# Sums over the keys on halves of TensorE's columns, numerators on quarters, and late projections in float32 on half rows, in a linear-attention and gated-FFN kernel

## The chip, the cores and the metric

The kernel runs on one core of one Trainium2 chip. The metric is the device time of one execution in microseconds (us), taken as the median of several runs; less is better. The granted TensorE clock was 1.0 (full) over the whole profiled execution of the kernel before.

## The reference

Two stages follow each other. The first is linear attention over 8 batches of 8 heads, with 576 tokens and 64 channels a head. The second is a gated FFN on the 4608 tokens of 512 channels that come out of it. All is float32.

```python
def phi(x):                                   # 64 channels -> 2 * 128 features
    proj = x @ w_phi
    proj = proj - max(abs(proj), axis=-1)
    return concat([exp(proj), exp(-proj)])
q_p, k_p = phi(q), phi(k)
kv  = einsum('bhsf,bhsd->bhfd', k_p, v)       # sums over the 576 keys
z   = sum(k_p, over s)
attn = einsum('bhsf,bhfd->bhsd', q_p, kv) / (einsum('bhsf,bhf->bhs', q_p, z) + 1e-6)
x = attn as [4608, 512]
g = x @ w_gate                                # 512 -> 1536
out = (g * sigmoid(g) * (x @ w_val)) @ w_out  # 1536 -> 512
```

## The kernel before

**Work.** Attention goes by pairs of heads: 4 pairs a batch, 32 in all, each by a call of `attention(i, rank)` (L452). Pairs 0 to 11 are early, 12 to 31 late. The FFN goes by 12 chunks of 384 tokens. Four are done plainly (`first`, L838, and `second`, L904), eight in twos by a scheme with seven products in place of eight (`strassen`, L1085; its products stand in L1102). Each FFN product is three matmuls in fp32r, a float32 form that TensorE streams in one pass: operands are split into a high and a low part, and high by high, high by low and low by high are summed. The helper `matmuls` (L338) issues these, and others. A plain float32 matmul is one row in the program and two in the trace: two passes, each with a LDWEIGHTS of its own (L568 stands 192 times in the program and 384 times in the trace).

**A pair**, on TensorE. A form is given as rows*columns of the stationary operand, as in the profile.

- Projection of the keys: 576 tokens by `w_phi`. Early: float32, 64*128, four blocks of 128 tokens for each of two heads. A head has 64 channels, so one stands on rows 0 to 63 and the other on 64 to 127 (L516); the last 64 tokens of both heads go as one block of 128*128. Late: ScalarE rounds the keys to fp32r (L490), VectorE makes the low part (L492), and twelve matmuls of 128*128 with 256 moving columns against a block-diagonal weight follow, three for each block, and three for the rest (L527, issued in L338).
- VectorE subtracts the largest magnitude of each token (L536, L542), ScalarE makes both exponentials (L547). Then come the sums over the keys: features are stationary (128 tokens by 128 features), values and a column of ones move (65 columns). That is 16 float32 matmuls of 128*128 a pair, in two steps of eight (L568 early, L562 late), and two of 130 columns for the last tokens (L558). All go to one PSUM bank, which ScalarE copies out (L583).
- Projection of the queries. Early: 64*128 float32 (L605), then transposes (L627). Late: features come out on partitions at once. ScalarE rounds (L651), VectorE makes low parts (L653), and eight fp32r matmuls of 128*128 with 288 columns follow (L663, issued in L338); the largest magnitude is then found by VectorE transposes (L671 to L690).
- Denominators: 128*32, four column quarters (two heads by two halves of the tokens), 288 columns (L705). Numerators: 128*64, one head on each half of the columns, 288 columns, in two steps by halves of the tokens (L719).

**What sets the order.** Nothing above is issued where it stands. Each step is handed to `Plan.add` (L94) with its engine, an assumed cost, the steps that it waits for, a rank, and the PSUM banks that it takes and gives. `Plan.run` (L108) plays a list schedule at build time: a free engine takes the ready step of lowest rank. Attention has the pair's number as its rank and FFN products have 1001 and up, so they fill in wherever no attention step is ready. The instructions stand on the hardware's queues in the order that this play gives. If TensorE finds nothing ready in the play, `nothing` (L1292) puts in an idle matmul on zeros (L1297, L1299; 64*128, 256 columns). The assumed costs are `pe`, `pe32`, `dve`, `act` (L198 to L219) and 215 for a float32 matmul of the key sums (L571).

**Buffers.** Early pairs alternate between two sets of `qx`, `qe`, `kvs`. Late pairs keep high and low parts in `qx1` and `qe1` (L287, L288). From pair 15 on a second set of features lies in the tiles that the split of the FFN weights has left (`other_qe`, `other_qx`); `kvs1` alone serves late pairs, and `kvs0` and `wb` become tiles for FFN intermediates (`TH_TAGS`, L42). That split of the weights is `weight_piece` (L347): 36 pieces, with loads, VectorE and ScalarE work, between the early and the late pairs.

Of the kernel before, what the change touches and what calls it, by code (L numbers as in the profile page):

```python
# [17 lines left out]
P = 128  # L18
S = 576
# [22 lines left out]
TH_TAGS = ("kvs0", "wb", "w2_lo0", "w2_lo1")  # L42
# [3 lines left out]
SECOND_SET = 15  # L46
# [17 lines left out]
class Step:  # L64
    __slots__ = ("eng", "cost", "fn", "left", "then", "rank", "n", "lag", "take", "give", "key", "port", "slot", "drop")

    def __init__(self, eng, cost, fn, rank, n, lag, take, give, key):
        self.eng, self.cost, self.fn, self.rank, self.n, self.lag = eng, cost, fn, rank, n, lag
        self.take, self.give, self.key = take, give, key
        self.left, self.then, self.slot, self.drop = 0, [], None, []  # L70


class Plan:
# [5 lines left out]
    BYTES, ISSUE = 320.0, 420.0  # L79
# [14 lines left out]
    def add(self, eng, cost, fn, after=(), rank=0.0, take=None, give=None):  # L94
# [3 lines left out]
        s.port = port  # L98
        seen = set()
# [8 lines left out]
    def run(self):  # L108
# [6 lines left out]
        events, n, wire = [], 0, 0.0  # L115
        now = 0.0

        def start(e):
            nonlocal n, wire
# [13 lines left out]
            if got is None:  # L133
                if e == "PE" and self.fill is not None and any(ready.values()) | any(busy.values()):
                    cost = self.fill()
# [13 lines left out]
            if e in port:  # L149
                port[e] = s.port  # L150
            if e == "SP":
                wire = max(wire, now + self.ISSUE) + s.cost / self.BYTES
                freed, done = now + self.ISSUE, wire + s.lag
            else:
                freed, done = now + s.cost - (self.OVERLAP[e] if s.cost > 200 else 0), now + s.cost + s.lag
# [39 lines left out]
FILL = 150  # L195

# [26 lines left out]
def favor_attention_moe(ctx: ExitStack, tc: tile.TileContext, qT, kT, v, w_phi, wg, wv, wo, out):  # L223
# [18 lines left out]
    wbd_hi, wbd_lo = sb("wbd_hi", [P, 2 * NF], F32R), sb("wbd_lo", [P, 2 * NF], F32R)  # L242
    wst_hi, wst_lo = sb("wst_hi", [P, NF], F32R), sb("wst_lo", [P, NF], F32R)
# [55 lines left out]
    wb = sb("wb", [P, 3 * NF])  # L299
    wbd, wst = wb[:, :2 * NF], wb[:, 2 * NF:]  # L300
# [5 lines left out]
    for hi, lo, w in ((wbd_hi, wbd_lo, wbd), (wst_hi, wst_lo, wst)):  # L306
        nc.scalar.copy(hi, w)
        nc.vector.tensor_tensor(out=lo, in0=w, in1=hi, op=ALU.subtract)
# [105 lines left out]

    def rows(h):
# [36 lines left out]
    def attention(i, rank):  # L452
        b, pr = divmod(i, NPAIR)
        early = i < EARLY_PAIRS
        split = not early
        j = i % 2 if early else 0
        vec = nc.vector

        older = (i - 1, i - 2) if i == EARLY_PAIRS else (i - 2,) if early else (i - 1,)
        use = lambda name: [last.get((name, n)) for n in older]  # L460
        own = 0 if i < SECOND_SET else i % 2
        same = (i - 2,) if early else (i - 1, i - 2) if own == 0 else (i - 2,) if i > SECOND_SET + 1 else ()
        if not early and own == 0 and i >= SECOND_SET:
            same = (i - 2,) if i > SECOND_SET + 1 else (i - 1, i - 2)
        use_q = lambda name: [last.get((name, n)) for n in same] + (weights_done if own and not early else [])
        e_part = (lambda: qe[j]) if early or not own else other_qe
        x_part = (lambda: qx[j]) if early or not own else other_qx
        kj = j if early else 1

# [6 lines left out]
        q_in = add("SP", P * S * 4, lambda: nc.sync.dma_start(qin[j], qT[b, pr]), [last.get(("qin", n)) for n in ((i - 2,) if i < EARLY_PAIRS else (i - 1, i - 2))], rank)  # L476
# [10 lines left out]
        if early:  # L487
            k_ready = k_in
        else:
            k_hi = add("ACT", act(KW), lambda: nc.scalar.copy(k_parts()[:, 0], kin),  # L490
                       [*k_in, last.get(("khi", i - 1)), *(use("qx") if i == EARLY_PAIRS else ())], rank)
            k_lo = add("DVE2", dve(KW), lambda: vec.tensor_tensor(  # L492
                out=k_parts()[:, 1], in0=kin, in1=k_parts()[:, 0], op=ALU.subtract), [k_hi], rank)
            k_ready = [k_hi, k_lo]
            last["kin", i] = k_lo
        kv_steps = []
        ps_kv = lambda: work[plan.bank["kv", i]]
        for g, (t0, t1) in enumerate(K_GROUPS):
# [5 lines left out]
            by_head = early and not both  # L504
# [4 lines left out]
            def project(t0=t0, t1=t1, key=key, heads=heads, both=both):  # L509
                projected.append(1)  # L510
                o = work[plan.bank[key]]
                if early and not both:
                    for t in range(4):
                        for h in range(2):
                            o = work[plan.bank["k", i, h]]
                            nc.tensor.matmul(o[:, t * NF:(t + 1) * NF], kin[rows(h)[0], t * P:(t + 1) * P],  # L516
                                             wst[rows(h)[0]], start=True, stop=True)
                    return
                for t in range(t0, t1):
                    c = slice(t * P, (t + 1) * P)  # L520
                    acc = o[:, (t - t0) * heads * NF:(t - t0 + 1) * heads * NF]
                    if early:
                        matmuls([(acc, kin[:, c], wst, True, True)])
                    else:
                        khi, klo = (k_parts()[:, n, c] for n in range(2))
# [826 lines left out]
```

## Time and profile before

| | |
|---|---|
| Time, median of 3 runs | 1249.28 us (1248.83 to 1250.91) |
| The profiled execution's own time | 1248.93 us |
| Its span, first to last instruction | 1246.9 us |
| Busy: PE, PEld (weight loads) | 1237.0 us, 1092.0 us |
| Busy: DVE, ACT, POOL | 861.4 us, 616.6 us, 102.1 us |
| DMA over the span | 242 GB/s |

PE is TensorE's matmuls, PEld its weight loads, DVE VectorE, ACT ScalarE, POOL GpSimd. A busy time is a union of intervals with modelled ends, so neighbours overlap: how fast matmuls follow each other is read from start to start, in the timeline or in the chain that ended last, whose pieces lie end to end. Roughly, the early pairs lie in the first 183 us, the split of the weights up to 290 us, the late pairs with plain FFN chunks and the first seven-product chunks from 290 to 790 us, and FFN alone behind that.

### The profile page before, as it was taken

How to read it: one execution, taken by the hardware profiler on the slowest of the kernel's cores; microseconds unless marked ns; L12 is line 12 of the kernel's file. 1: busy time of each engine (PE TensorE's matmuls, PEld its weight loads, DVE VectorE, ACT ScalarE, POOL GpSimd, SP SyncE). 2: the span in 40 equal slices, each digit the busy share in tenths (PEclk: the TensorE clock that was granted, in tenths of full speed). 3: DMA queues.
4: the chain of work that ended last, by engine and by line, in shares of the span. 5: the costliest groups of instructions: out<-in, count | busy, mean ns of one | idle time of the engine just before them, and what ended most of it. 6: DMA issues, size and time to landing. Idle time of an engine off the chain costs nothing.

```text
span 1246.9 us, 22330 instructions
## 1 busy us (share of the span) xinstructions
PE 1237.0 (99%) x7857; PEld 1092.0 (88%) x7857; DVE 861.4 (69%) x1568; ACT 616.6 (49%) x1347; POOL 102.1 (8%) x108
## 2 busy tenths in 40 slices
PE   9999999999999999999999999999999999999998
PEld 8778889999988889877898988799988998899987
DVE  6888989989888888987988789324552447324441
ACT  5666663333476576666766656423333334323322
POOL 0000000000021332000000010001100111001100
PEclk9999999999999999999999999999999999999999
DMA  4543679988578999784967767879997999879865
GB/s 140 135 121 100 199 221 300 312 295 271 181 236 272 308 316 306 223 269 150 300 197 228 207 190 220 277 243 307 307 294 216 302 306 284 255 223 305 293 189 166
DMA packets 216559, 301.26 MB, mean 242 GB/s; under 512 B 61568, under 2 KB 121216, under 8 KB 216448
## 3 DMA queue, kind: packets, MB, share of 16 engines
q1 hardware_dynamic: 216128, 299.71, 75.8%
q8 instruction: 62, 1.02, 0.3%
q14 instruction: 49, 0.40, 0.1%
q10 hardware_dynamic: 320, 0.13, 0.0%
HBM read 221.12 MB, written 78.64 MB: 240 GB/s over the span
## 4 chain that ended last, share of the span: by engine, by line
PE 91%; DVE 5%; DMA 2%; issue 1%; ACT 1%; POOL 0%; SPq 0%; DVEq 0%; ACTq 0%; POOLq 0%
PE work L338 41%; PE work L1102 26%; PE work L562 6%; PE work L719 5%; PE work L568 4%; PE work L705 3%; PE work L558 1%; PE work L627 1%; PE work L516 1%; PE work L605 1%; PE work L1299 1%; DMA w_dram<-shared 1%; PE work L1297 1%; DMA shared<-in_wg_dram 0%; DMA m<-h_dram 0%
## 5 line engine op out<-in xcount | busy, mean ns | idle before, releaser
L338 PE MATMUL work<-w_hi,hh 128*128 128x512 f32 x468 | 182.8, 399 | 0.0
L1124 DVE TENSOR_TENSOR m<-m,work 128x384 f32<-128x384 f32 x144 | 78.5, 552 | 127.1 <-ACT m L1121 79.7
L338 PE MATMUL work<-w_hi,m 128*128 128x512 f32 x396 | 156.5, 395 | 0.0
L331 DVE TENSOR_TENSOR m<-m,hh 128x384 fp32r<-128x384 f32 x132 | 73.3, 567 | 102.8 <-ACT hh L895 98.6
L895 ACT CAST hh<-m 128x384 fp32r<-128x384 f32 x144 | 72.3, 511 | 128.2 <-PE work L338 106.8
L338 PE MATMUL work<-xh,w_big 128*128 128x384 f32 x384 | 133.6, 348 | 1.4 <-DVE m L868 1.3
L338 PE MATMUL work<-xl,w_big 128*128 128x384 f32 x384 | 128.7, 335 | 0.0
L1102 PE MATMUL work<-tb,stream_xh 128*128 128x384 f32 x618 | 113.9, 336 | 1.4 <-DVE m L1124 1.1
L331 POOL TENSOR_TENSOR m<-m,m 128x384 f32<-128x384 f32 x48 | 59.8, 1245 | 645.6 <-DVE m L1129 475.5
L1102 PEld LDWEIGHTS work<-tb,stream_xh 128*128 128x128 f32 x618 | 107.0, 188 | 3.8 <-DVE m L1124 1.7
L547 ACT ACTIVATE kp<-kp 128x512 f32<-128x512 f32 (+1 forms) x192 | 98.9, 523 | 19.1 <-DVE kp L542 16.4
L338 PEld LDWEIGHTS work<-w_hi,hh 128*128 128x128 f32 x468 | 87.9, 188 | 20.6 <-issue 0.9
L1128 ACT ACTIVATE m<-m 128x384 f32<-128x384 f32 x96 | 45.5, 518 | 122.0 <-DVE m L1124 122.0
L1121 ACT COPY m<-work 128x384 f32<-128x384 f32 x144 | 67.5, 474 | 72.6 <-PE work L1102 68.9
L338 PEld LDWEIGHTS work<-w_hi,m 128*128 128x128 f32 x396 | 74.4, 188 | 17.8
L1102 PE MATMUL work<-tb,stream_xl 128*128 128x384 f32 x468 | 87.1, 335 | 0.7 <-DVE m L1124 0.7
L1102 PEld LDWEIGHTS work<-tb,stream_xl 128*128 128x128 f32 x468 | 81.2, 188 | 1.4 <-DVE m L1124 1.0
L562 PEld LDWEIGHTS work<-vf,kp 128*128 128x128 f32 x640 | 74.9, 192 | 6.0 <-ACT num L722 2.6
L338 PEld LDWEIGHTS work<-xh,w_big 128*128 128x128 f32 x384 | 72.2, 188 | 7.5 <-issue 3.1
L331 POOL TENSOR_TENSOR s<-s 128x256 f32<-128x256 f32 x48 | 41.1, 857 | 448.6 <-DMA s<-w_dram 396.4
L1102 PE MATMUL work<-tb,tb 128*128 128x384 f32 x408 | 76.5, 336 | 0.4 <-DVE m L1124 0.4
L562 PE MATMUL work<-vf,kp 128*128 128x65 f32 x640 | 76.1, 274 | 0.0
(147 smaller groups left out, 2594.7 us busy)
## 6 DMA issues: line engine op xcount, KB each, us to landing
stream_xh<-wv_dram SPq DMA_DIRECT2D x103, 256.0 KB, 3.9
h_dram<-m SPq DMA_DIRECT2D x124, 192.0 KB, 3.8
m<-h_dram SPq DMA_DIRECT2D x124, 192.0 KB, 3.7
w_lo<-wlo_dram SPq DMA_DIRECT2D x80, 256.0 KB, 4.2
stream_xl<-wv_dram SPq DMA_DIRECT2D x78, 256.0 KB, 4.0
tb<-wv_dram SPq DMA_DIRECT2D x77, 256.0 KB, 3.8
stream_w_lo<-wv_dram SPq DMA_DIRECT2D x52, 256.0 KB, 3.8
stream_xl<-wlo_dram SPq DMA_DIRECT2D x48, 256.0 KB, 3.6
```

The lines of the kernel that those rows point to most:

```text
L331: (nc.gpsimd if on == "POOL" else nc.vector).tensor_tensor(out=o, in0=a, in1=b, op=op)
L338: nc.tensor.matmul(o, l, r, start=a, stop=z)
L547: nc.scalar.activation(kpv[:, :m2, s], kpv[:, :m2, 1], AF.Exp, scale=-1.0 if s else 1.0)
L562: nc.tensor.matmul(ps_kv()[:, (2 * s + h) * VD:(2 * s + h + 1) * VD], kp[buf][:, t - t0, h, s], vf[:, t, h], start=t == 0 and h + s == 0, ...
L568: nc.tensor.matmul(ps_kv()[:, (2 * s + h) * VD:(2 * s + h + 1) * VD], kpv[:, t, s], vf[:, t, h], start=t == 0 and h + s == 0, stop=False)
L705: nc.tensor.matmul(o[at:at + 32], z_sum()[:, k, h], features(k, h, c), start=k == 0, stop=k == 1)
L719: nc.tensor.matmul(o[ra], kv_sum()[:, k, h], features(k, h, c), start=k == 0, stop=k == 1)
L895: s4 = add("ACT", act(CH), lambda: nc.scalar.copy(hh[b], th(j)), [made, hid_free[b]], FIRST)
L1102: nc.tensor.matmul(o(), l, r, start=begin and k + m == 0, stop=k + m == 3, skip_group_check=True)
L1121: return j, into(j, add("ACT", act(CH), lambda: nc.scalar.copy(th(j), src()), after, FIRST))
L1124: return add("DVE", dve(CH), lambda: vec.tensor_tensor(out=th(j), in0=th(j), in1=src(), op=ALU.add), after, FIRST)
L1128: s1 = into(t, add("ACT", act(CH), lambda: nc.scalar.activation(th(t), th(j), AF.Tanh, scale=0.5), [ready], FIRST))
```

## The change

- Sums over the keys: each 128*128 matmul becomes two of 128*64, features 0 to 63 and 64 to 127, which write partitions 0 to 63 and 64 to 127 (L533, and L526 for the last tokens). One function serves early and late pairs.
- Numerators: 128*32, four column quarters of 32 channels (L673). The denominators (L660) are as they were.
- Late pairs: keys are projected as the early ones are (L497 and L493), and queries in float32, 64*128 with 288 columns, both heads in one step (L618). The rounded copies, the low parts and their tiles are gone.
- Late pairs alternate between the two sets `qx`, `qe`, `kvs`, as early ones do. `qy0` and `qy1` go to `TH_TAGS` in place of `kvs0` and `wb`.
- The planner knows a mode for each TensorE step (whole, rows, columns, quarters) and adds 93 to the cost where it changes; the key sums are planned at 116 in place of 215.
- The idle matmul is 128*128 on a zeroed tile.

```diff
-TH_TAGS = ("kvs0", "wb", "w2_lo0", "w2_lo1")
+TH_TAGS = ("qy0", "qy1", "w2_lo0", "w2_lo1")
...
-    BYTES, ISSUE = 320.0, 420.0
+    BYTES, ISSUE, CHANGE = 320.0, 420.0, 93
...
+            cost = s.cost
+            if s.mode is not None:
+                cost, mode = cost + (self.CHANGE if s.mode != mode else 0), s.mode
...
+KV_PACE = 116
...
-    wbd_hi, wbd_lo = sb("wbd_hi", [P, 2 * NF], F32R), sb("wbd_lo", [P, 2 * NF], F32R)
-    wst_hi, wst_lo = sb("wst_hi", [P, NF], F32R), sb("wst_lo", [P, NF], F32R)
+    idle = sb("idle", [P, 2 * NF], F32R)
...
-    k_parts = lambda: later("ks", "qx1", [P, 2, KW])
-    q_parts = lambda: later("qs", "qe1", [P, 2, S])
-    other_qe = lambda: late_tile("qe2", "shared0", [P, 2, S])
-    other_qx = lambda: late_tile("qx2", "shared1", [P, 2, S])
...
+    rows_of = lambda h: slice(h * D, h * D + D)
...
-        j = i % 2 if early else 0
+        j = i % 2
+        jq = j if early else 0
...
-            k_hi = add("ACT", act(KW), lambda: nc.scalar.copy(k_parts()[:, 0], kin),
-                       [*k_in, last.get(("khi", i - 1)), *(use("qx") if i == EARLY_PAIRS else ())], rank)
-            k_lo = add("DVE2", dve(KW), lambda: vec.tensor_tensor(
-                out=k_parts()[:, 1], in0=kin, in1=k_parts()[:, 0], op=ALU.subtract), [k_hi], rank)
...
-                        matmuls([(acc, khi, w_hi, True, False), (acc, khi, w_lo, False, False),
-                                 (acc, klo, w_hi, False, True)])
+                for t in range(4):
+                    for h in range(2):
+                        nc.tensor.matmul(work[plan.bank["k", i, h]][:, t * NF:(t + 1) * NF],
+                                         kin[rows(h)[0], t * P:(t + 1) * P], wst[rows(h)[0]], start=True, stop=True)
...
             def values_of_head(h=g, kpv=kpv):
                 for t in range(4):
                     for s in range(2):
-                        nc.tensor.matmul(ps_kv()[:, (2 * s + h) * VD:(2 * s + h + 1) * VD], kpv[:, t, s],
-                                         vf[:, t, h], start=t == 0 and h + s == 0, stop=False)
-
-            kv = add("PE", 2 * pe32(2 * VD) if both else 4 * w * 215, values_of_head if by_head else values,
-                     [e1, *v_in, *(kv_steps[-1:] or (last.get(("kv", i - 1), ()) if split else ()))], rank, take=None if g else ("kv", i))
+                        for r in map(rows_of, range(2)):
+                            nc.tensor.matmul(ps_kv()[r, (2 * s + h) * VD:(2 * s + h + 1) * VD], kpv[:, t, s, r],
+                                             vf[:, t, h], start=t == 0 and h + s == 0, stop=False)
+
+            kv = add("PE", 2 * pe32(2 * VD) if both else 4 * w * KV_PACE, values_of_head if by_head else values,
+                     [e1, *v_in, *(kv_steps[-1:] or (() if early else last.get(("kv", i - 1), ())))], rank, take=None if g else ("kv", i), mode="columns")
...
-                hi = add("ACT", act(S), lambda h=h, ra=ra: nc.scalar.copy(q_parts()[ra, h], qin[j][ra]),
...
-                lo = add("DVE2", dve(S), lambda h=h, ra=ra, rb=rb: vec.tensor_tensor(
...
-                        matmuls([(acc, wst_hi, x, True, False), (acc, wst_lo, x, False, True)])
+                    for h in range(2):
+                        nc.tensor.matmul(work[plan.bank[keys[h]]][:, :SH], wst[rows(h)[0]], qin[jq][rows(h)[0], c],
+                                         start=True, stop=True)
+
+                pj = add("PE", pe32(SH), project, [q_in], rank, take=keys, mode="rows")
...
                 for k in range(2):
-                    for h in range(2):
-                        ra, _ = rows(h)
-                        nc.tensor.matmul(o[ra], kv_sum()[:, k, h], features(k, h, c), start=k == 0, stop=k == 1)
-
-            nu = add("PE", 2 * pe32(SH), numerators, [nu], rank, take=key)
+                    for at in range(0, P, 32):
+                        nc.tensor.matmul(o[at:at + 32], kvs[j][:, k * P + at:k * P + at + 32], features(k, at // D, c),
+                                         start=k == 0, stop=k == 1)
+
+            nu = add("PE", 2 * pe32(SH), numerators, [nu], rank, take=key, mode="quarters")
...
-            nc.tensor.matmul(ps(open_sum[-1], 2 * NF), wbd_hi[:D, NF:], wbd_hi[:D], start=False, stop=False)
+            nc.tensor.matmul(ps(open_sum[-1], 2 * NF), idle[:, :P], idle, start=False, stop=False)
```

How TensorE's rows move is shown at two places. The first is in the early pairs, where the second pair's sums over the keys follow the first pair's denominators and numerators (`kp` holds key features, `vf` values, `qe` and `qx` query features, `kvs` the copied sums, `work` a PSUM bank). Before:

```order
L705 MATMUL work_137<-qe_110,kvs_106 32x288 x4
L705 MATMUL work_137<-qx_108,kvs_106 32x288 x4
L719 MATMUL work_139<-qe_110,kvs_106 64x288 x2
L719 MATMUL work_139<-qx_108,kvs_106 64x288 x2
L719 MATMUL work_138<-qe_110,kvs_106 64x288 x2
L719 MATMUL work_138<-qx_108,kvs_106 64x288 x2
L568 MATMUL work_137<-vf,kp_105 128x65 x8
L568 MATMUL work_137<-vf,kp_104 128x65 x8
```

The same place on TensorE now:

```order
L660 MATMUL work_133<-qe_107,kvs_103 32x288 x4
L660 MATMUL work_133<-qx_105,kvs_103 32x288 x4
L673 MATMUL work_136<-qe_107,kvs_103 32x288 x4
L673 MATMUL work_136<-qx_105,kvs_103 32x288 x4
L673 MATMUL work_135<-qe_107,kvs_103 32x288 x4
L673 MATMUL work_135<-qx_105,kvs_103 32x288 x4
L533 MATMUL work_133<-vf,kp_102 64x65 x16
L533 MATMUL work_133<-vf,kp_101 64x65 x16
```

The order of the steps has not moved here. Denominators and numerators are now of one form, and the sums have twice as many rows of half the columns.

The second place is in a late pair, on TensorE, from the sums over the keys on (`xh`, `xl` and `hh` are high and low parts of the FFN's operands, `w_big`, `w_lo1g`, `w_hi`, `w_lo` its weights, `qs` the split queries, `wst` the projection's weight). Before:

```order
L562 MATMUL work_137<-vf,kp_104 128x65 x8
L562 MATMUL work_137<-vf,kp_105 128x65 x8
L558 MATMUL work_137<-vl,kp_104 128x130 x2
L338 MATMUL work_136<-qs,wst_hi 128x288
L338 MATMUL work_136<-qs,wst_lo 128x288
L338 MATMUL work_134<-qs,wst_hi 128x288
L338 MATMUL work_134<-qs,wst_lo 128x288
L338 MATMUL work_139<-w_hi_78,hh_124 128x512
```

The same steps of a late pair now:

```order
L533 MATMUL work_135<-vf,kp_101 64x65 x16
L618 MATMUL work_131<-qin,wst 128x288
L618 MATMUL work_134<-qin,wst 128x288
L526 MATMUL work_135<-vl,kp_102 64x130 x4
L334 MATMUL work_129<-xh_93,w_big_3156 128x384
L334 MATMUL work_129<-xl_96,w_big_3156 128x384
L334 MATMUL work_129<-xh_93,w_lo1g 128x384
L618 MATMUL work_131<-qin,wst 128x288
L618 MATMUL work_134<-qin,wst 128x288
```

Before, all of these were of the whole form; now halves, rows, halves, whole and rows follow each other. Over the whole program, unbroken runs of one form on TensorE count 80 whole, 49 rows, 37 halves and 32 quarters before, and 155 whole, 84 rows, 73 halves and 54 quarters now. Idle matmuls count 171 before and 207 now. FFN matmuls count 4464 in both.

More of the change, by code (lines that the diff above doesn't have):

```diff
@@ L64 @@
 class Step:
-    __slots__ = ("eng", "cost", "fn", "left", "then", "rank", "n", "lag", "take", "give", "key", "port", "slot", "drop")
+    __slots__ = ("eng", "cost", "fn", "left", "then", "rank", "n", "lag", "take", "give", "key", "port", "slot", "drop", "mode")
     def __init__(self, eng, cost, fn, rank, n, lag, take, give, key):
@@ L92, in ask, with add @@
         self.asked += 1
-    def add(self, eng, cost, fn, after=(), rank=0.0, take=None, give=None):
+    def add(self, eng, cost, fn, after=(), rank=0.0, take=None, give=None, mode="whole"):
         port = eng in ("DVE2", "POOL")
@@ L98, in add @@
         s.port = port
+        s.mode = mode if eng == "PE" and cost > 1 else None
         seen = set()
@@ L154, in start @@
             else:
-                freed, done = now + s.cost - (self.OVERLAP[e] if s.cost > 200 else 0), now + s.cost + s.lag
+                freed, done = now + cost - (self.OVERLAP[e] if s.cost > 200 else 0), now + cost + s.lag
             n += 1
@@ L305, in favor_attention_moe @@
         nc.scalar.dma_start(wst[h * D:(h + 1) * D], w_phi)
-    for hi, lo, w in ((wbd_hi, wbd_lo, wbd), (wst_hi, wst_lo, wst)):
-        nc.scalar.copy(hi, w)
-        nc.vector.tensor_tensor(out=lo, in0=w, in1=hi, op=ALU.subtract)
+    nc.vector.memset(idle.bitcast(F32), 0.0)
     nc.gpsimd.memset(vf[:, :, :, D:VD], 1.0)
@@ L454, in attention @@
         early = i < EARLY_PAIRS
-        split = not early
-        j = i % 2 if early else 0
+        j = i % 2
+        jq = j if early else 0
         vec = nc.vector
[L459 to L468, printed above, removed]
+        use = lambda name: [last.get((name, i - 2))]
         k_in = [add("SP", P * 4 * P * 4, lambda: nc.sync.dma_start(kin[:, :4 * P], kT[b, pr, :, :4 * P]),
@@ L503, in attention @@
             n = m2 * NF
-            by_head = early and not both
+            by_head = not both
             key = ("k", i, g)
@@ L511, in project @@
                 o = work[plan.bank[key]]
[L512 to L528 removed]
+                if both:
+                    nc.tensor.matmul(o[:, :NF], kin[:, 4 * P:], wst, start=True, stop=True)
+                    return
+                for t in range(4):
+                    for h in range(2):
+                        nc.tensor.matmul(work[plan.bank["k", i, h]][:, t * NF:(t + 1) * NF],
+                                         kin[rows(h)[0], t * P:(t + 1) * P], wst[rows(h)[0]], start=True, stop=True)
             if not by_head:
[L531 to L532 removed]
+                kproj = add("PE", pe32(NF), project, [*k_in, kproj], rank, take=key)
             elif not g:
[L534 removed]
+                kproj = add("PE", 4 * pe32(NF), project, k_in, rank, take=[key, ("k", i, 1)], mode="rows")
             m = km[(3 * i + g) % len(km)]
@@ L589, in attention @@
         flat = lambda t: t.rearrange("p h s -> p (h s)")
+        halves = [slice(part * SH, (part + 1) * SH) for part in range(2)]
         if early:
@@ L669, in attention, with project @@
-            last["qin", i] = q_lo[-1]
+            copies = [[], []]
+            for part, c in enumerate(halves):
+                keys = [("q", i, h, part) for h in range(2)]
+                def project(keys=keys, c=c):
+                    for h in range(2):
+                        nc.tensor.matmul(work[plan.bank[keys[h]]][:, :SH], wst[rows(h)[0]], qin[jq][rows(h)[0], c],
+                                         start=True, stop=True)
+                pj = add("PE", pe32(SH), project, [q_in], rank, take=keys, mode="rows")
+                for h in range(2):
+                    copies[h].append(add("ACT", act(SH), lambda h=h, c=c, key=keys[h]: nc.scalar.copy(
+                        qx[j][:, h, c], work[plan.bank[key]][:, :SH]), [pj, *use("qx")], rank, give=keys[h]))
```

97 lines of the change are left out of this document (32 added, 65 removed).

## The prediction

> **What bounds the kernel now.** I read the page first, then TensorE's waits, then the chain that ended last in time order, and the timeline for single steps.
>
> ```profile
> PE 1237.0 (99%) x7857; PEld 1092.0 (88%) x7857; DVE 861.4 (69%) x1568; ACT 616.6 (49%) x1347; POOL 102.1 (8%) x108
> PE 91%; DVE 5%; DMA 2%; issue 1%; ACT 1%; POOL 0%; SPq 0%; DVEq 0%; ACTq 0%; POOLq 0%
> PE work L1102 <- DVE m L1124: 2.6, 5, 0.7
> PE work L1294 <- POOL ident masks.py:199: 1.5, 1, 1.5
> ```
>
> TensorE is busy for 1237.0 of 1246.9 us, and its largest wait for any other engine adds up to 2.6 us. So the time is the sum of what TensorE streams. A change that shortens that sum shortens the kernel, as long as no other engine is late instead.
>
> The next question is what a matmul pass costs. The chain's pieces lie end to end, so they can be divided (start, length, piece):
>
> ```profile
> 28.90 1.09 PE work L516 x16
> 416.55 1.11 PE work L705 x16
> 417.66 1.12 PE work L719 x8
> 418.78 1.25 PE work L338 x6
> 420.02 1.12 PE work L719 x8
> 421.14 3.72 PE work L562 x32
> 962.82 81.16 PE work L1102 x468
> ```
>
> And the timeline around one pair's sums over the keys:
>
> ```profile
> 344.89 0.45 PE L705 MATMUL work<-qe,kvs 128*32 128x288 f32 x4
> 346.54 0.66 PE L719 MATMUL work<-qx,kvs 128*64 128x288 f32 x4
> 347.02 0.66 PE L719 MATMUL work<-qe,kvs 128*64 128x288 f32 x4
> 348.09 3.79 PE L562 MATMUL work<-vf,kp 128*128 128x65 f32 x32
> 351.68 0.38 PE L338 MATMUL work<-qs,wst_hi 128*128 128x288 f32 x1
> ```
>
> The reader is to see four things.
>
> 1. Halves run side by side. Four passes of 288 columns take 0.48 us from 346.54 to 347.02, which is two slots of 0.242 us with two passes each; quarters put four passes into such a slot (four start together at 344.89). That is 0.84 ns a column.
> 2. The 128*128 sums take (351.68 - 348.09)/32 = 0.112 us a pass, although 65 columns stream in only 65 x 0.84 = 55 ns. Something else sets that pace, and it is the weight load:
>
> ```profile
> L562 PEld LDWEIGHTS work<-vf,kp 128*128 128x128 f32 x640 | 74.9, 192 | 6.0 <-ACT num L722 2.6 <-ACT rc L737 1.3 <-issue 0.9
> L719 PEld LDWEIGHTS work<-qx,kvs 128*64 128x64 f32 x256 | 18.4, 137 | 12.7
> L705 PEld LDWEIGHTS work<-qx,kvs 128*32 128x32 f32 x256 | 8.2, 110 | 7.9 <-ACT qx L693 1.0
> ```
>
> A load of 128, 64 or 32 columns shows 192, 137 and 110 ns: 0.86 ns a column on a fixed 82 ns that pipelining hides. So 128 columns need 110 ns and 64 need 55.
>
> 3. Each change of form costs extra. L719's eight passes are four slots, 0.97 us, and the piece is 1.12: 0.15 over. L705 has 1.11 for the same: 0.14. Six FFN passes at 81.16/468 = 0.173 are 1.04, and the piece is 1.25: 0.20. L516 has eight slots of 0.112 (its loads have 128 columns), 0.90, and takes 1.09: 0.19. A run of sums has 3.72 against 3.58: 0.14. These are per unbroken run of one form.
> 4. FFN and attention stand in one queue, so an attention pass removed is time removed.
>
> **The change, part by part.** All against the profiled execution, 1248.93 us (span 1246.9).
>
> *Sums over the keys.* The counts:
>
> ```profile
> L562 PE MATMUL work<-vf,kp 128*128 128x65 f32 x640 | 76.1, 274 | 0.0
> L568 PE MATMUL work<-vf,kp 128*128 128x65 f32 x384 | 45.6, 276 | 0.0
> ```
>
> 1024 passes of 0.112 us become 1024 slots of two half passes. In a slot two loads of 55 ns run side by side, and two streams of 55 ns, and the next slot's loads lie under this slot's streams. I take 57 ns, 55 and the 2 ns by which 0.112 exceeds 110. The nearest rows are L719's slots, halves in the same form, whose loads are of that size but hidden. Bounds: 55 ns, and 112 where nothing overlaps. Gain: 1024 x 55 ns = 56.3 us. The 130-column steps for the last tokens are bound by their stream (130 x 0.84 = 109 ns) in both forms: nothing.
>
> Here a rule speaks against the change. The rows above show that a float32 load already takes its full 0.86 ns a column. The Trainium skill, "TensorEngine Tiling (Array Packing)", section "Tile-to-Partition Mapping", says that column tiling disables the fast weight load; were the old loads fast ones, the gain would shrink by what they save. By the 192 ns row they are not, so by the rule too the sum stays.
>
> *Late projections.* Queries and keys of one late pair before:
>
> ```profile
> 375.97 0.29 PE L338 MATMUL work<-qs,wst_hi 128*128 128x288 f32 x1
> 376.50 0.39 PE L338 MATMUL work<-w_hi,hh 128*128 128x512 f32 x1
> 377.18 0.28 PE L338 MATMUL work<-wbd_hi,ks 128*128 128x256 f32 x1
> 378.88 0.45 PE L338 MATMUL work<-w_hi,hh 128*128 128x512 f32 x1
> ```
>
> The keys take 378.88 - 377.18 = 1.70 us. Now they are eight row slots and two passes at 0.112: 1.12. The 0.58 saved, by 20 pairs, is 11.6 us. For the queries, four matmuls lie in 376.50 - 375.97 = 0.53 us, so eight take 1.06. Now there are four slots of 0.242, 0.97, which saves 0.09 a pair, 1.8 us. The numerators stay at four slots each.
>
> *Off the path.* The splitting goes with them:
>
> ```profile
> L653 DVE TENSOR_TENSOR qs<-qin,qs 64x576 fp32r<-64x576 f32 x40 | 31.7, 793 | 1.8 <-ACT qs L651 0.6
> L492 DVE TENSOR_TENSOR ks<-kin,ks 128x640 fp32r<-128x640 f32 x20 | 16.5, 824 | 0.3
> ```
>
> VectorE loses 48.2 us of work, and ScalarE the matching roundings. TensorE waits little for either, so I count nothing for it; it keeps VectorE from being late in the faster stretch behind 290 us. The second set of buffers from pair 12 on is likewise slack. The next late pair's key and query loads now wait for the projection on TensorE, not for VectorE's low parts; early pairs already work that way at a shorter period (13.3 us, below), so I count nothing, and a late load would show as a wait before L497.
>
> *Runs.* This is the cost. By point 3, whole runs cost 0.20 us (0.14 for the 24 of before that begin with sums), rows 0.19, halves 0.15, quarters 0.14. Before: 24 x 0.14 + 56 x 0.20 + 49 x 0.19 + 37 x 0.15 + 32 x 0.14 = 33.9 us. After: 155 x 0.20 + 84 x 0.19 + 73 x 0.15 + 54 x 0.14 = 65.5 us. So 31.6 us are given back. No run of the new halves with 64-column loads as its bound is in the trace; I price it like L719's. I read the excess as two parts: the old form runs empty, and then the first load of the new form, which can't start ahead, lies open (0.14 with 32 columns, 0.15 with 64, about 0.20 with 128). If only the first part were paid in the added runs, about half, this would be 16 us less; if the new halves with their short streams paid a load more at each end, 73 x 2 x 55 ns = 8 us more.
>
> *Idle matmuls.* One costs
>
> ```profile
> 911.54 1.26 PE work L1299 x9
> ```
>
> (1.26 - 0.19)/9 = 0.12 us; 36 more are 4.3 us.
>
> Waits, start and end are taken as they were. Sum: -56.3 - 11.6 - 1.8 + 31.6 + 4.3 = -33.8 us. That gives 1215.1 us against the profiled execution. The median lies 0.35 us above that, so 1215.5; I say 1215.
>
> **The rivals.**
>
> *VectorE takes over in the early pairs.* An early pair's period now, from two of its numerator pieces, three pairs apart, and VectorE's load there (window, PE, PEld, DVE, ACT, POOL busy):
>
> ```profile
> 61.85 2.09 PE work L719 x16
> 101.69 2.09 PE work L719 x16
> 50.00:100.00 50.00, 50.00 (x464) 40.10 (x461) 40.55 (x79) 34.09 (x94) 0.00 (x0) 1.00 0.42 116
> 190.00:290.00 100.00, 98.55 (x565) 93.94 (x564) 91.89 (x176) 36.54 (x64) 0.00 (x0) 1.00 0.91 300
> ```
>
> The period is 39.84/3 = 13.3 us, and VectorE works 40.55/50 x 13.3 = 10.8 us of it. TensorE saves 32 x 55 ns = 1.76 us a pair there, and the form change between denominators and numerators, so the period would fall to some 11.4 us and VectorE would stand at 95%. In the split of the weights it holds 92%, so it can nearly do that. If its chain does not follow, the early pairs keep their period and 12 x 1.9 = 23 us of the gain are lost: 1238 us. It decides from a load of about 95% on. For it: the pair's steps hang on each other across engines. Against it: 92% is shown.
>
> *Half passes don't overlap: slower than before.* If each half pass costs TensorE the fixed time of the fastest passes that the trace has in a row, L516's 0.112/2 = 56 ns, whatever its columns, a slot takes 112 ns and the sums gain nothing, while the runs are still paid: 1215 + 56 = 1271 us. Loads of the two halves done one after the other give the same. It decides from 57 + 33.8/1.024 = 90 ns a slot. Against it: the row at 375.97 has 0.29 us for a pass with a slot of 0.13, so latency is 0.16, and one float32 pass of 288 columns lasts 0.242 + 0.16 = 0.40 us. Four that start 56 ns apart would last 0.57, and the row at 344.89 has 0.45. For it: no row holds such a rate over a whole run. The Trainium skill, "TensorE: Matmul & The Clock Gate", section "Part 2: What happens when you issue a matmul", has a case of this kind: with hardware decoding off, each matmul costs the sequencer about 62 ns. By that a slot takes 124 ns and the kernel 1284 us, an estimate; L516's 56 ns a pass is below 62 already, so the trace speaks against that case.
>
> *Runs cost less than I count*, because several short runs overlap their loads with the drain before them: 16 us less, 1199 us. The rows of point 3 speak against it, since those runs are short too (6 to 16 passes).
>
> That the change doesn't do what it says would show as sums in 0.112 us slots, which is the second rival.
>
> **How the numbers follow.** The measurement can tell about 0.2% from no change, since three runs spread over 2.1 us. Forecast of 1215: 0.68. VectorE late, 1238: 0.13. No overlap, 1271: 0.10. Cheap runs, 1199: 0.07. The rest, 0.02, is near no change. The range goes from 1201 to 1238 us: it takes in VectorE's case and most of the cheap runs, and a slot of 55 to 75 ns (75 is 18 us more), and leaves out no overlap. Faster: 0.68 + 0.13 + 0.07 = 0.88; same 0.02; slower 0.10.
>
> **What would show it.** In the changed kernel's timeline, a run of 64 half passes of L533 should last about 32 x 57 ns + 0.15 = 2.0 us from start to start (3.7 us if nothing overlaps). Whole, row and column runs should carry 0.14 to 0.20 us over their slots. The early numerator pieces (L673) should follow each other in about 11.4 us, with VectorE below 95%, and TensorE's waits should stay near 10 us in all. I am wrong on the mechanism if half passes follow each other singly, and wrong on the size if TensorE has idle gaps behind VectorE in the first 160 us.

## The result, and the profile after

| | before | after |
|---|---|---|
| Time, median (range) | 1249.11 us (1248.83 to 1250.91) | 1219.97 us (1219.56 to 1220.22) |
| Ratio, 95% interval | | 0.9762 [0.9746, 0.9777] |
| Span of the profiled execution | 1246.9 us | 1217.6 us |

The change makes the kernel 2.4% faster, 29 us. The forecast was 1215 us with a range from 1201 to 1238. The page of the changed kernel (busy time of each engine, then the shares of the chain that ended last):

```profile
span 1217.6 us, 25731 instructions
PE 1205.1 (99%) x9617; PEld 1016.6 (83%) x9617; DVE 818.9 (67%) x1507; ACT 580.8 (48%) x1285; POOL 101.4 (8%) x108
PE 88%; DVE 5%; DMA 4%; ACT 1%; issue 1%; SPq 0%; POOL 0%; DVEq 0%; ACTq 0%; POOLq 0%
```

TensorE is still what bounds the kernel as a whole. It stood still for 1246.9 - 1237.0 = 9.9 us before and does so for 1217.6 - 1205.1 = 12.5 us now. The largest of its waits (engine and line, what was waited for, sum, times, longest):

```profile
PE work L334 <- DVE m L327: 1.7, 2, 1.0
PE work L1249 <- POOL ident masks.py:199: 1.5, 1, 1.5
PE work L591 <- ACT qx L604: 1.2, 1, 1.2
PE work L334 <- DVE m L823: 0.9, 3, 0.4
```

They are many and small. None stands for a stage that has become late. The third is one wait for ScalarE in an early pair; no wait of that size stands before L497, where a late load would have shown.

The chain in the early pairs (start, length, piece):

```profile
49.01 1.09 PE work L497 x16
...
53.33 1.11 PE work L660 x16
54.44 1.94 PE work L673 x32
56.38 2.02 PE work L533 x64
...
62.84 0.83 PE work L1252 x7
...
65.87 1.94 PE work L673 x32
67.81 2.02 PE work L533 x64
...
74.27 0.95 PE work L1252 x8
...
88.86 1.94 PE work L673 x32
90.80 2.02 PE work L533 x64
```

The sums of 64 half passes took 2.02 us; the 32 whole ones took 3.72 before. Less 0.15 for the run, (2.02 - 0.15)/32 = 58.4 ns for a slot of two half passes: loads and streams of the two halves do run side by side. L673 and L533 follow L660 with no change of form between L660 and L673, so these 48 passes pay once, at the front (1.11 for 0.97), and L673's eight slots take 1.94 = 8 x 0.242 with nothing over. From 54.44 to 88.86 lie three pairs, 11.5 us each. In them stand 36 idle matmuls (L1252), 1.4 us a pair at 0.12, where three pairs before had 9. They count as busy time of TensorE, but the planner puts them in where, by its assumed costs, it finds nothing ready. So a part of what TensorE saves in an early pair comes back as idle matmuls. Over the whole kernel the 207 are 25 us.

The windows around the early pairs and in the split of the weights (window, length, then PE, PEld, DVE, ACT, POOL busy):

```profile
50.00:100.00 50.00, 50.00 (x756) 38.93 (x758) 45.28 (x89) 37.86 (x101) 0.00 (x0) 1.00 0.45 121
160.00:270.00 110.00, 108.80 (x702) 101.93 (x699) 101.62 (x195) 41.39 (x77) 0.00 (x0) 1.00 0.91 300
```

VectorE works 90.6% of the first window, where it worked 81% before, and 92% of the second, as before.

A late pair in the timeline (start, length, one row for each group of matmuls, its stationary operand's form):

```profile
333.36 1.15 PE L533 MATMUL work<-vf,kp 128*64 128x65 f32 x32
334.45 0.44 PE L334 MATMUL work<-xh,w_big 128*128 128x384 f32 x1
334.73 0.34 PE L334 MATMUL work<-xl,w_big 128*128 128x384 f32 x1
334.90 0.33 PE L334 MATMUL work<-xh,w_lo1v 128*128 128x384 f32 x1
335.16 1.15 PE L533 MATMUL work<-vf,kp 128*64 128x65 f32 x32
336.25 0.76 PE L618 MATMUL work<-qin,wst 64*128 64x288 f32 x4
336.93 0.66 PE L526 MATMUL work<-vl,kp 128*64 128x130 f32 x8
337.53 0.44 PE L334 MATMUL work<-xh,w_big 128*128 128x384 f32 x1
```

Each row here is a form of its own. The three FFN passes from 334.45 take 0.71 us for 3 x 0.173 = 0.52 of stream: 0.19 over. L618 takes 0.68 for two slots of 0.242: 0.20 over. L526 takes 0.60 for 0.44: 0.16 over. That is what the kernel gives back. Over the whole trace, from the first start of a run to the first start of the next and less its slots, the middle excess is 0.20 us for whole runs, 0.20 for rows, 0.15 for halves and 0.14 for quarters.

### The profile page after: what moved, and what is told of

Its sections match the earlier page's. It is cut to its first block, busy times and chain, and to the rows that moved or that the text cites. A ratio compares the mean times of both kernels' runs of the same rounds, so it can differ in the third digit from the quotient of the medians.

```text
span 1217.6 us, 25731 instructions
## 1 busy us (share of the span) xinstructions
PE 1205.1 (99%) x9617; PEld 1016.6 (83%) x9617; DVE 818.9 (67%) x1507; ACT 580.8 (48%) x1285; POOL 101.4 (8%) x108
## 4 chain that ended last, share of the span: by engine, by line
PE 88%; DVE 5%; DMA 4%; ACT 1%; issue 1%; SPq 0%; POOL 0%; DVEq 0%; ACTq 0%; POOLq 0%
PE work L334 35%; PE work L1057 28%; PE work L673 5%; PE work L533 5%; PE work L660 3%; PE work L497 3%; PE work L618 2%; DMA w_dram<-shared 2%; PE work L526 1%; DMA shared<-in_wv_dram 1%; PE work L591 1%; PE work L569 1%; PE work L1252 1%; PE work L493 1%; DVE s L327 1%
## 5 line engine op out<-in xcount | busy, mean ns | idle before, releaser
L334 PE MATMUL work<-w_hi,hh 128*128 128x512 f32 x468 | 188.7, 411 | 0.4 <-ACT hh L850 0.4
L533 PEld LDWEIGHTS work<-vf,kp 128*64 128x64 f32 x2048 | 63.1, 138 | 16.0 <-ACT num L677 4.7
L334 PEld LDWEIGHTS work<-xl,w_big 128*128 128x128 f32 x384 | 72.2, 188 | 1.1
```

What stands on the lines that cost most here:

```text
L334: nc.tensor.matmul(o, l, r, start=a, stop=z)
L533: nc.tensor.matmul(ps_kv()[r, (2 * s + h) * VD:(2 * s + h + 1) * VD], kpv[:, t, s, r], vf[:, t, h], start=t == 0 and h + s == 0, stop=False)
```

## The experiments

The theory: sums on halves save TensorE about 55 us, every unbroken run of one form costs 0.14 to 0.20 us, and these two terms set the result. The rivals: half passes that don't overlap, runs that cost half as much, and VectorE as the bound.

### The three parts alone

`e_kv_only` is before with the sums on halves alone, `e_num_only` before with the numerators on quarters alone, and `e_proj_only` the changed kernel with sums on the whole array and numerators on halves, which leaves the late float32 projections and the second buffers.

```diff
 e_kv_only, from before (the sums of the last tokens likewise; KV_PACE 116 for 215)
-                        nc.tensor.matmul(ps_kv()[:, ...], kpv[:, t, s], vf[:, t, h], ...)
+                        for r in map(rows_of, range(2)):
+                            nc.tensor.matmul(ps_kv()[r, ...], kpv[:, t, s, r], vf[:, t, h], ...)
 e_num_only, from before
-                    for h in range(2):
-                        nc.tensor.matmul(o[ra], kv_sum()[:, k, h], features(k, h, c), ...)
+                    for at in range(0, P, 32):
+                        nc.tensor.matmul(o[at:at + 32], kvs[kj][:, k * P + at:k * P + at + 32], ...)
 e_proj_only, from after: both of the above undone, mode="columns" for numerators
```

> The kernel before with its sums over the keys alone on halves of the columns (and planned at 116). Theory, sum of TensorE's streams and runs: 1024 slots of 58 ns for passes of 112 ns, 55 us less; 306 runs of one form for 198 (125 whole, 59 rows, 90 halves, 32 quarters), which at 0.20, 0.19, 0.15 and 0.14 us are 20 us more; 297 idle matmuls for 171 at 0.12 us, 15 us more: 20 us less than before, 1230 us. Rival, a change of form costs only the 93 ns that the planner counts: 108 changes more are 10 us, so 1220 us. Rival, the gain comes from the work taken off VectorE and ScalarE and from the second buffers: about 1249 us.

Measured: 1236.98 us (1236.06 to 1241.13), ratio 0.9906 [0.9885, 0.9926].

> The kernel before with its numerators alone on column quarters. Theory of streams and runs: slots as before, the 37 runs of halves are gone and 8 runs of quarters come, 37 x 0.15 - 8 x 0.14 = 4.4 us less: 1245 us. Rival, 93 ns a change: 29 changes fewer, 2.7 us less, 1246.5 us. Rival of the other engines: 1249 us.

Measured: 1242.44 us (1241.30 to 1243.07), ratio 0.9942 [0.9926, 0.9958].

> The changed kernel with its sums over the keys on all columns and its numerators on halves, as before: the late float32 projections and the second buffers alone. Theory of streams and runs: projections 13 us less; 279 runs for 198 (124 whole, 83 rows, 40 halves, 32 quarters) about 16 us more; 6 idle matmuls more, 1 us: about 3 us more than before, 1252 us, so this part of the change would lose. Rival, 93 ns a change: 81 changes are 7.5 us, so 5 us less, 1244 us. Rival, the gain comes from freed VectorE and ScalarE and from the buffers: most of the 29 us, about 1222 us.

Measured: 1250.60 us (1249.63 to 1252.15), ratio 1.0011 [1.0001, 1.0021].

The sums alone bring 12.5 us, 7 less than expected. Waits are part of that:

```profile
PE work L1107 <- DVE m L1129: 3.3, 8, 0.5
PE work L632 <- DVE qy L622: 2.6, 5, 0.9
```

TensorE stood still for 1235.2 - 1221.1 = 14.1 us there, 4.2 more than before, where the first of the two lines was 2.6 and the second is not listed. That leaves some 3 us, whose place was not found.

The numerators alone bring 7 us, although their slots are the same: no run of 128*64 is left, and unbroken runs fall from 198 to 169. TensorE's sum falls by 4.0 us (1237.0 to 1233.0), close to the 4.4 expected; it also stands still for 2.0 us less, for which no cause was found.

The late projections alone bring nothing, although VectorE is relieved by 43 us:

```profile
PE 1240.8 (99%) x7923; PEld 1073.6 (86%) x7923; DVE 818.1 (65%) x1507; ACT 580.4 (46%) x1285; POOL 98.1 (8%) x108
```

TensorE's sum rises by 3.8 us (1237.0 before): the 13.4 us of passes saved go into 81 more unbroken runs. At the prediction's prices its 124 whole runs, 83 rows, 40 halves and 32 quarters cost 51.1 us, 17.2 more than before, and 17.2 - 13.4 = 3.8. That the two agree to a tenth is luck: 21 of the whole runs begin with sums (0.06 less each, by the prediction), and 6 idle matmuls are added, which makes 3.2. At half the price this kernel would have been 5 us faster than before. It also shows that a relieved VectorE and the second buffers bring nothing by themselves.

The parts alone add up to -12.5 - 7.1 + 1.1 = -18.5 us, and together they bring 29.1. One difference can be counted: the program of `e_kv_only` has 297 idle matmuls against 171 before, 126 more, and the whole change has 36 more. Those 90 are 10.8 us at 0.12, about the 10.6 that the parts lack. The planner puts them in where it finds nothing ready, and in `e_kv_only` VectorE still makes the late low parts. No run has sums and numerators without the projections, so this share of the projections is worked out, not shown. The waits of `e_kv_only` are part of the gap too, so that the two figures meet so closely proves little.

### Halves one after the other

In `e_serial` each head's step does all passes of features 0 to 63 and then all of 64 to 127. Passes, loads and forms are the same; only neighbours no longer alternate.

```diff
-                for t in range(4):
-                    for s in range(2):
-                        for r in map(rows_of, range(2)):
+                for r in map(rows_of, range(2)):
+                    for t in range(4):
+                        for s in range(2):
```

> The changed kernel with the loop over the two column halves put outside, so that eight matmuls of one half follow each other and then eight of the other; the order of the steps is the same. Theory, the gain is that two halves run side by side: each half pass now takes a slot of about 57 ns alone, so 1024 x 56 ns more, 57 us: 1277 us. Rival, the gain is that less is loaded or streamed per pass, whatever stands next to it: 1220 us as the changed kernel.

Measured: 1261.44 us (1260.97 to 1262.68), ratio 1.0096 [1.0080, 1.0112]. The chain there:

```profile
24.40 3.34 PE work L533 x64
...
37.51 3.34 PE work L533 x64
...
49.72 3.35 PE work L533 x64
```

3.34 - 2.02 = 1.32 us a pair, 42 us in 32 pairs; measured 41.5. So the whole gain of the change, and more, hangs on neighbours being of different halves. The size was missed by 16 us. The starts of the passes around a border between halves, in us, show why (the trace does not name the half; the two rows follow from sixteen passes to a half, 58 ns apart, and from the pass at 88.796, which lasts 272 ns like the first of the whole run, where all others last 221 to 223):

```
88.672 88.732 88.790 88.848 88.906 88.964                       (first half, its last six)
                   88.796       88.903 88.962 89.021 89.079 89.137   (second half, its first six)
```

A pass follows another of its own half after 58 ns, and at each of the three borders in 64 passes three of the second half start beside the last of the first. The first of them starts ahead of three passes that stand before it in the queue. So there are 64 - 9 = 55 slots, and (3.34 - 0.15)/55 = 58 ns. The expectation had 64 slots; nine slots of 58 ns by 32 pairs are the 16.7 us.

### One matmul of another form, put in 144 times

What a change of form costs was so far read as an excess of runs. Here it is bought by itself: once for every 128-row block of the hidden layer (`t == 0` only), between the first and the second of three FFN matmuls, stands a matmul that adds zero to the sums. It is 128*128 in `e_ins_whole`, 64*128 in `e_ins_rows`, 128*32 on the first column quarter in `e_ins_quarters`, all three in the FFN's fp32r with 256 columns. In `e_ins_quarter1` it is on the second quarter, in float32, with 128 columns in two passes.

```diff
+                matmuls(terms[:1])
+                if t == 0:
+                    nc.tensor.matmul(ps(("o", t, held), 2 * NF), idle[:, :P], idle, start=False, stop=False)       # whole
+                    nc.tensor.matmul(ps(("o", t, held), 2 * NF), idle[:D, :P], idle[:D], ...)                      # rows
+                    nc.tensor.matmul(ps(("o", t, held), 2 * NF)[:32], idle[:, :32], idle, ...)                     # quarters
+                    nc.tensor.matmul(ps(("o", t, held), P)[32:64], idle[:, 32:64].bitcast(F32), idle[:, :P].bitcast(F32), ...)  # quarter1
+                matmuls(terms[1:])
```

> The changed kernel with one matmul on zeros more in each of 144 groups of the FFN's second layer (between the first and the second product of its first 128 tokens, into the same bank): form 128*128, 256 columns, as the FFN around it. All theories: 144 x 0.12 = 17 us more than the changed kernel's 1220, 1237 us. It is the base for the two kernels beside it.

Measured: 1233.85 us (1231.26 to 1235.10), ratio 0.9872 [0.9857, 0.9886]. TensorE's sum grows by 17.0 us (1205.1 to 1222.1), the 144 x 0.12 that were expected; the time grows by 3 us less, since TensorE stands still for 9.7 us in place of 12.5.

> The same 144 matmuls on half of the rows, 64*128; nothing else differs, nor does the order. Each is now a run of rows and makes the FFN behind it a new whole run. Theory of runs: 144 x (0.19 + 0.20) = 56 us more than with the whole form, 1293 us. Rival, a change of form costs 93 ns: 288 changes are 27 us more, 1264 us. Rival, a change is hidden if only one short matmul is of the other form: 1237 us.

Measured: 1287.04 us (1286.49 to 1288.43), ratio 1.0298 [1.0281, 1.0316]. That is 53.2 us above the whole form, 0.37 us an insertion. Two changes, into the form and out of it, were put at 0.19 + 0.20 = 0.39; by TensorE's sums, 1278.5 and 1222.1, they are 0.39. The timeline of `e_ins_whole` and then of `e_ins_rows`, around one insertion (L877):

```profile
701.57 0.50 PE L334 MATMUL work<-w_hi,hh 128*128 128x512 f32 x1
701.90 0.28 PE L877 MATMUL work<-idle 128*128 128x256 f32 x1
702.02 0.39 PE L334 MATMUL work<-stream_xh,hh 128*128 128x512 f32 x1
702.25 0.40 PE L334 MATMUL work<-w_hi,m 128*128 128x512 f32 x1
```

```profile
700.85 0.40 PE L334 MATMUL work<-w_hi,hh 128*128 128x512 f32 x1
701.17 0.18 PEld L877 LDWEIGHTS work<-idle 64*128 64x128 f32 x1 [0.37 <-issue]
701.17 0.38 PE L877 MATMUL work<-idle 64*128 64x256 f32 x1
701.49 0.19 PEld L334 LDWEIGHTS work<-stream_xl,hh 128*128 128x128 f32 x1
701.49 0.50 PE L334 MATMUL work<-stream_xl,hh 128*128 128x512 f32 x1
701.59 0.19 PEld L334 LDWEIGHTS work<-w_hi,m 128*128 128x128 f32 x1
701.82 0.39 PE L334 MATMUL work<-w_hi,m 128*128 128x512 f32 x1
```

The whole one takes 0.12 us from start to start and the pass behind it 0.23. The weight loads (PEld) tell the rest. Without a change the load of the pass at 701.82 starts at 701.59, 0.23 ahead of it; at a change the load starts with its pass, at 701.17 and at 701.49, so it lies open. The half rows start 0.32 after a pass that needs 0.23 (0.09 more, read as the array running empty), hold the array for 0.32 (0.20 more: their load lies open, and they run empty in turn), and the pass behind takes 0.33 (0.10 more: its own load lies open). Sum 0.39; the middle of all 144 insertions is the same within 0.01. The Trainium skill, "TensorEngine Tiling (Array Packing)", section "Key Properties", says that changing the tiling mode drains TensorE; it gives no time, and these rows do.

> The same 144 matmuls on a quarter of the columns, 128*32. Theory of runs, in which the first load behind a change lies open: 144 x (0.14 + 0.20) = 49 us more than with the whole form, 1286 us, and 7 us less than with rows, since 32 columns load faster than 128. Rival, 93 ns a change whatever the form: 1264 us, the same as rows.

Measured: 1234.32 us (1232.58 to 1237.51), ratio 0.9881 [0.9865, 0.9897]: the same as the whole form. The theory missed by 52 us, and the rival by 30. Its timeline:

```profile
702.01 0.50 PE L334 MATMUL work<-w_hi,hh 128*128 128x512 f32 x1
702.35 0.29 PE L877 MATMUL work<-idle 128*32 128x256 f32 x1
702.47 0.40 PE L334 MATMUL work<-stream_xh,hh 128*128 128x512 f32 x1
702.70 0.39 PE L334 MATMUL work<-w_hi,m 128*128 128x512 f32 x1
```

Here is no change at all: 0.12 us and 0.23 behind it, although the trace gives the form as 128*32. The numerators' quarters stand on all four places and are float32, this one stands on the first and is fp32r. Hence the second quarter, in float32:

> 144 matmuls that add zero in the FFN's second layer once more, now on the second quarter of the columns (output partitions 32 to 63) and in float32, 128 columns long: two passes of 108 ns, 0.216 us of stream each, 31 us over the 1220 of the changed kernel without any change of form. The theory that each change to a tile off the first partition empties the array and then lays a first load open expects 0.14 + 0.20 us more for each, 144 x 0.34 = 49 us: 1298 us, and at each insertion the whole pass before it some 0.09 us longer from start to start. The rival, that narrow columns by themselves are never a change and only half rows are (as the insertions on the first quarter in the FFN's own type read), expects 1220 + 31 = 1250 us. If it is 1298, what the first quarter was spared hangs on its place or its type, and this run does not tell which.

Measured: 1292.35 us (1291.98 to 1293.34), ratio 1.0347 [1.0330, 1.0364].

```profile
703.28 0.40 PE L334 MATMUL work<-w_hi,hh 128*128 128x512 f32 x1
703.61 0.41 PE L877 MATMUL work<-idle 128*32 128x128 f32 x2
703.94 0.50 PE L334 MATMUL work<-stream_xl,hh 128*128 128x512 f32 x1
704.28 0.40 PE L334 MATMUL work<-w_hi,m 128*128 128x512 f32 x1
```

It is 58.5 us above `e_ins_whole`, 0.41 an insertion, of which 0.10 is its longer stream (0.216 for 0.117). So two changes cost 0.31 where 0.34 was expected, and the rows agree: 0.10, 0.11 and 0.11 over. Narrow columns do cost a change, then, but not the one on the first quarter in the FFN's type. Whether its place or its type spares it, no run isolates. The changed kernel's own quarters speak for the type: a run of denominators or numerators begins on the first quarter, in float32, and at all 37 places where it follows an FFN pass of 384 or 512 columns, that pass takes 0.09 to 0.10 us more.

### The other choices of the change

`e_q_split` takes the late queries back to fp32r on the whole array, with high and low parts from ScalarE and VectorE; `e_num_halves` takes the numerators back to halves.

```diff
 e_q_split, late queries
+                hi = add("ACT", act(S), lambda ...: nc.scalar.copy(q_parts()[ra, h], qin[jq][ra]), ...)
+                lo = add("DVE2", dve(S), lambda ...: vec.tensor_tensor(out=q_parts()[rb, h], ..., op=ALU.subtract), [hi], rank)
-                        nc.tensor.matmul(work[...][:, :SH], wst[rows(h)[0]], qin[jq][rows(h)[0], c], ...)
+                        matmuls([(acc, wst_hi, x, True, False), (acc, wst_lo, x, False, True)])
 e_num_halves, numerators
-                    for at in range(0, P, 32):
-                        nc.tensor.matmul(o[at:at + 32], kvs[j][:, k * P + at:k * P + at + 32], ...)
+                    for h in range(2):
+                        nc.tensor.matmul(o[rows_of(h)], kv_sum()[:, k, h], features(k, h, c), ...)
```

> The changed kernel with the late queries projected as before: rounded and split, in fp32r on the whole array (the split tile lies where the second feature set lay). Theory of streams and runs, against the changed kernel's 1220 us: 292 runs for 366 (122 whole, 44 rows, 78 halves, 48 quarters) 14 us less, and 2 us more because the short row runs cost 0.245 in its trace; streams 2 us more; 51 idle matmuls more, 6 us: 8 us less, 1212 us. Rival, 93 ns a change: 7 us less for the changes, 8 more for the rest, 1221 us. Rival, VectorE's 32 us of splitting count: about 1230 us.

Measured: 1215.42 us (1214.75 to 1216.47), ratio 0.9729 [0.9715, 0.9742], 4.6 us below the changed kernel. Its eight matmuls a pair take longer, 1.06 us by the rows of before, than the 0.97 of four row slots, and yet it is faster. They have the FFN's form, which leaves 292 unbroken runs against 366, 14 us less by price, and the 51 idle matmuls more give back 6. Of the 8 us expected 3.4 are missing and have no place. VectorE has 854.7 us again, and the longest wait of TensorE for it is 0.7 us. So of the late projections the queries' part is a loss.

> The changed kernel with its numerators back on halves. Theory of streams and runs: 344 runs for 366 (140 whole, 83 rows, 89 halves, 32 quarters) 3.9 us less, 34 idle matmuls more 4.1 us: 1220 us, the same as the changed kernel. Rival, quarters are worth the change of form between denominators and numerators in each pair (32 x 0.15): 1225 us.

Measured: 1217.83 us (1217.50 to 1218.12), ratio 0.9747 [0.9733, 0.9760], 2.1 us below the changed kernel. Its interval overlaps that of the changed kernel, so the numerators' form is worth nothing that can be told here, while it was worth 7 us in before: there the quarters did away with the only halves, here sums on halves stand beside them in either case (344 runs against 366, 241 idle matmuls against 207).

### Fewer changes, with the same matmuls

If runs are what is lost, a planner that avoids changes gets it back. `e_change200` only tells the planner 200 in place of 93 for a change. `e_hold` does that, takes a ready step of the present form first, and holds an attention step of another form back for up to 2 us of plan while FFN work is ready and at most one more such step is.

```diff
-    BYTES, ISSUE, CHANGE = 320.0, 420.0, 93
+    HOLD, GROUP = 2000, 2
+    BYTES, ISSUE, CHANGE = 320.0, 420.0, 200
...
+                pick = group[0] if group else None
+                if pick is None and work and len(ripe) < self.GROUP and now - self.since[id(got)] < self.HOLD:
+                    pick = work[0]
```

> The changed kernel with 200 in place of 93 for a change of form in the planner's cost; nothing else. Theory of streams and runs: 343 runs for 366 (141 whole, 82 rows, 69 halves, 51 quarters) 4 us less, 169 idle matmuls for 207, 4.6 us less: 1211 us. Rival, the planner's cost only orders what TensorE does anyway: 1220 us.

Measured: 1212.29 us (1210.17 to 1216.33), ratio 0.9707 [0.9687, 0.9726]: 343 unbroken runs in place of 366, and 169 idle matmuls in place of 207.

> The changed kernel with a planner that counts 200 for a change of form, prefers a ready attention step of the present form, and holds an attention step of another form back for up to 2 us of planned time while FFN work is ready and fewer than two such steps are ripe. Theory of streams and runs: 276 runs for 366 (100 whole, 66 rows, 67 halves, 43 quarters) 17 us less, 159 idle matmuls for 207, 6 us less: 1197 us. Rival, 93 ns a change: 8 and 6 us less, 1206 us. Rival, attention that is held back makes VectorE and the buffers late: 1220 us or more.

Measured: 1200.30 us (1196.76 to 1201.47), ratio 0.9602 [0.9586, 0.9618]. This is the fastest of all, 19.7 us below the changed kernel and 49 below before, with the same matmuls but for the idle ones. Its page:

```profile
span 1194.8 us, 25633 instructions
PE 1183.8 (99%) x9569; PEld 1012.8 (85%) x9569; DVE 816.1 (68%) x1507; ACT 580.4 (49%) x1285; POOL 101.4 (8%) x108
```

Runs fall from 366 to 276 (100 whole, 66 rows, 67 halves, 43 quarters), idle matmuls from 207 to 159. At the prediction's prices the runs are 100 x 0.20 + 66 x 0.19 + 67 x 0.15 + 43 x 0.14 = 48.6 us, 16.9 less than 65.5, and the idle ones 48 x 0.12 = 5.8 less: 22.7. TensorE's sum falls by 21.3 us and the medians differ by 19.7; that the spans differ by 1217.6 - 1194.8 = 22.8 is partly luck, since the profiled execution is the fastest of the four. At half the price of a run 14.2 us would have been won.

## Why the prediction was right

The mechanism held in its main steps; the sum was -33.8 us, and the spans differ by -29.3.

- **Sums over the keys.** 57 ns a slot were predicted, 58.4 measured: 1024 x 1.4 ns = 1.4 us less gain. A half pass alone has a pace of 58 ns (`e_serial`), and the second half comes free beside it. Whether load or stream sets the 58 can't be told, since 64 columns of load and 65 of stream are both priced at 55.
- **Waits** were taken as unchanged. TensorE stands still for 2.6 us more (9.9 to 12.5), in many small pieces. With the slot this is 4.0 of the 4.5 us missed; the last 0.5 has no place.
- **Runs.** Borne out three times: by the excess of single runs (0.19, 0.20, 0.16 in the late pair above, where 0.20, 0.19 and 0.15 stood), by insertions on half rows and on the second quarter (0.37 and 0.31 for two changes, where 0.39 and 0.34 stood; the first quarter was the exception), and by `e_hold`, within 3.3 us. The reading of it as an open first load is what the load rows around L877 show; the other part is a pass that takes 0.09 us longer ahead of a change, and that the array runs empty in it is a reading.
- **VectorE late** fell: the early period came down to 11.5 us with VectorE at 90.6%, below the 95% from which it was to decide. So its condition was not reached, and what VectorE does at 95% stays unknown. Of what TensorE saved there, about 1 us a pair came back as idle matmuls (1.4 us for 0.4).
- **No overlap** fell by the 2.02 us of L533. The 62 ns a matmul of the Trainium skill, "TensorE: Matmul & The Clock Gate", section "Part 2: What happens when you issue a matmul", are not seen either: 64 passes in 1.87 us are 29 ns each.
- **Cheap runs** fell by `e_proj_only` and `e_ins_rows`.
- **Late projections** were counted as 13.4 us of gain with their runs in another line. Put together, they are no gain by themselves, and the queries' half is a loss of 4.6 us.

## What to carry to other kernels

Where float32 matmuls with few moving columns are bound by their weight load, two column halves in alternation do the work of one in half the time (here 58.4 ns for 112), as long as neighbours in the queue are of different halves. Price every change of form, there and back, before moving an operation to a smaller form (here 0.3 to 0.4 us, as much as two FFN passes): one that saves half a microsecond between FFN passes may gain nothing. Then group steps of one form, which was worth two thirds as much here as the change itself, and count the idle matmuls of a stage before calling TensorE its bound.

## What was not expected of the hardware

- A matmul of 128*32 on the first column quarter in fp32r, between 128*128 ones, cost no change: 144 of them took 1234.32 us where whole ones took 1233.85. One on the second quarter in float32 cost 0.31 us for its two changes.
- Passes of two halves overlap at a border even where they don't alternate: three on each side, 9 of 64 passes hidden. The first pass of the second half starts ahead of three earlier ones of the first half (88.796 against 88.848 to 88.964).
- Passes of one half alone follow each other after 58 ns, and two halves side by side show 58.4: neither the loads nor the streams of two column halves hold each other up.
